# A list scheduler's margins, the place of the sine tables and a second engine for the first scalings, in a one-core attention, Fourier-mix and feed-forward kernel

## The chip, the cores and the metric

The kernel runs on one core of a Trainium2 chip. The metric is device time in microseconds (us) of one execution of the whole program. Three executions of the kernel before took 598.55, 597.87 and 601.43 us; the median is 598.55.

## The reference, cut to what matters

Eight batches, twelve heads, 448 tokens, head size 64 (model width 768), hidden width 3072, all float32. Attention uses normalised queries and keys and a temperature of 0.1. Its output goes through a two-dimensional Fourier transform of which the real part is added, a layer norm and a two-layer feed-forward part.

```python
q_n = q / (np.linalg.norm(q, axis=-1, keepdims=True) + 1e-06)
k_n = k / (np.linalg.norm(k, axis=-1, keepdims=True) + 1e-06)
attn = softmax(np.matmul(q_n, k_n.transpose(0, 1, 3, 2)) / tau)
x = (attn @ v).transpose(0, 2, 1, 3).reshape(8, 448, 768)
mixed = np.real(np.fft.fft(np.fft.fft(x, axis=1), axis=2))
u = x + mixed
un = (u - mean(u)) / np.sqrt(var(u) + 1e-06)
out = u + np.maximum(un @ w_ch1, 0.0) @ w_ch2
```

## The kernel before, in words

**Stages of a batch.** The program treats the batches one after another, with the attention of the next batch laid between the feed-forward matmuls of the present one. For a batch b:

- Loads. q and k come through the SP queue (line 646 for batches 0 and 1, line 772 into three staging buffers `STG` for the others), v through GpSimd's own queue (lines 829 to 832), and the weights w1 and w2 in 24 pieces through GpSimd's queue too (`W1b`, `W2b`, lines 578 and 579), at most three in flight: each waits for the third piece before it.
- Norms. ScalarE squares (`sq`, lines 653 and 781), VectorE sums per head (`ss`, 657 and 783), ScalarE takes the root as Ln and Exp (`ln`, `nrm`, 597 and 599), VectorE adds 1e-6 and takes the reciprocal (`eps`, `rcp`, 600 and 601). Then the scaling (`sc`): in batches 0 and 1 by VectorE (lines 679 and 683), from batch 2 on by GpSimd (line 790). In batches 0 and 1 TensorE transposes (`tk`, `tq`, `tt`, lines 707 to 732) and ScalarE or VectorE copies to `KT`, `QT`, `KTD` (`ek`, `eq`, `et`, lines 698 and 742); from batch 2 on DMA transposes do it on the SP queue (line 796), and `ktd` (a copy, line 1359 or 1360) and `qdup` (GpSimd, 821) follow them.
- Attention, in six pairs of heads. Scores by TensorE (`qk`, lines 869, 881, 882), exponentials by ScalarE (`ex`, 849; 24 instructions in batch 0), products with v (`pv`, 900 and 906), then on VectorE the reciprocal of the sums (`rd`, 924) and the product (`x`, 926).
- Fourier part. Sums and differences on VectorE (`fa`, `f`, `g`, lines 943 to 972), the transform over tokens on TensorE with a table `CSs` (and in batch 0 its negative `CSn`; `fs`, lines 988 and 993), copies (`te`, 1004 and 1005), the transform over the model width with a table `CSd` (`fd`, 1031), the additions (`u`, 1059) and the layer norm (`bs`, `ba`, `ln2`, `rs`, `un`, lines 1088 to 1097).
- Feed-forward. `h` (line 1163) and, after the relu copies (`relu`, 1179), the products with w2 (line 1194), the sums (1214 to 1226) and the stores.

**The tables.** `consts` makes the angles. Those for `CSs` are made first, on VectorE, and ScalarE turns them into sines at once (`sins`: 450 columns twice, lines 556 and 559), with the trigonometric function set loaded before anything else (line 349). The set with Ln and Exp is loaded right after the second square of batch 0 (`ldt0`, line 656). Two rows of `CSs` are halved by GpSimd (`half`, line 810) and `CSn` is made by VectorE (`sinn`, line 813). The angles of the larger table `CSd` are GpSimd's work (`tpd`, `tqd`, `trd`, `tad`, lines 504, 541, 546, 548) with a last step on VectorE (`tmd`, line 549). Its sines come after the last exponential of batch 0: the trigonometric set is loaded a second time, three sines follow (lines 556 to 559), and then the other set again (line 563).

**What sets the order.** Each engine runs its own instruction stream in order. The streams are written by a list scheduler in the program (`Plan.schedule`). Each step has a duration, a priority and its dependences; the scheduler takes the step that can start first by its own model of the engines and of the transfers (`FLOW`, `drain`), and by priority among equals. `SHIFT` adds hand-found numbers to the priorities of named steps. `rtime` gives the earliest start of a step: the end of each dependence, plus a fixed latency, plus the step's `margin`, which counts where TensorE takes the step or where the dependence is a transfer. `qk` has a margin of 0.3, `pv`, `fs` and `fd` of 0.2, the squares from batch 2 on of 1.0. `PIECE` and `PORT` model that a VectorE step of certain names waits for a piece of a GpSimd step that runs beside it. The model only sets the order; on the chip each step waits for the semaphores of its dependences.

**Fillers.** Where TensorE has a gap in the plan, `fill` puts in matmuls whose result is not used (line 1403), six at a time.

Of the kernel before, what the change touches and what calls it, by code (L numbers as in the profile page):

```python
# [13 lines left out]
DM = H * DH  # L14
# [23 lines left out]
    "ex3_0": {1: -3.7}, "tpd": {0: 1193.6}, "trd": {0: -57.8, 1: -108.8}, "tad": {0: -35.6, 1: -94.8}, "u1_0": {1: -264.8, 3: 72.4, 4: 79.2},  # L38
# [29 lines left out]
}  # L68

PIECE = {r"sc[KQ]\d_1": 0.95, r"scT\d_1": 0.42, r"sc\d_\d": 0.6, r"f[avm]\dp_\d": 0.54, r"t\d\d": 0.94}
PORT = r"eps\d|f[a01]\d_\d|g\d_\d|u\d+_\d|un\d_\d|s\d\d_\d|t\d\d|sc[KQT]\d_\d"

class Op:
# [1385 lines left out]
```

## Time and profile before

| | us |
|---|---|
| Median of three executions | 598.55 |
| The profiled execution, its own time | 598.88 |
| Its span, first to last instruction | 597.1 |
| TensorE busy, fillers included | 574.5 |
| Fillers (line 1403) before and after 53.15 us | 17.65 and 5.54 |
| First feed-forward matmul (line 1163) starts at | 53.15 |

The span lies 1.8 us below the profiled execution's own time. Times inside the profile are counted from the start of the span. In rows of the timeline the first number is the start, the second the duration, and a bracket at the end says how long the engine was idle before it and on whom it waited. PE is TensorE, PEld its weight load, DVE VectorE, ACT ScalarE, POOL GpSimd and SP the sync engine with its queue.

### The profile page before, as it was taken

The page shows a single profiled execution, that of the slowest core. Times are in us where ns is not written, and L with a number is a line of the kernel's source. Part 1 is how long each engine was busy: PE and PEld are TensorE (multiplying, and loading weights), DVE is VectorE, ACT ScalarE, POOL GpSimd, SP SyncE. Part 2 cuts the span into 40 slices and gives each one's busy share as a digit, 9 for nine tenths or more (in the row PEclk, how much of TensorE's full clock was granted, in tenths as well). Part 3 has the DMA queues.
Part 4 walks back from the last instruction along what each step waited for, and adds up shares of the span by engine and source line. Part 5 has one row for each costly group of instructions (what it writes and reads, how often), then busy time and mean ns, then how long its engine had stood idle before and what let it go on. Part 6 is the DMA issues. An engine that isn't in the chain of part 4 may idle for free.

```text
span 597.1 us, 15228 instructions
## 1 busy us (share of the span) xinstructions
PE 574.5 (96%) x6250; PEld 448.1 (75%) x6250; DVE 418.9 (70%) x976; ACT 354.8 (59%) x678; POOL 213.0 (36%) x324
## 2 busy tenths in 40 slices
PE   5889979999999999999999999999999999999997
PEld 4679867678678687678778688778668688778684
DVE  6968878898878776887788768865768556841222
ACT  7975878447867775468646676348745564124140
POOL 7843412732364264521460426341541210300302
PEclk9989999999999999999999999999999999999999
DMA  9999994964299349564592249373191210140001
GB/s 213 148 255 163 184 203 84 169 131 93 60 167 154 42 121 133 120 121 101 94 163 56 56 126 145 103 120 74 30 150 41 43 54 1 45 76 16 40 16 53
DMA packets 187638, 62.14 MB, mean 104 GB/s; under 512 B 166704, under 2 KB 185392, under 8 KB 187568
## 3 DMA queue, kind: packets, MB, share of 16 engines
q1 hardware_dynamic: 129648, 38.35, 34.1%
q0 software_dynamic: 57920, 22.81, 29.8%
q8 instruction: 49, 0.80, 0.6%
q14 instruction: 21, 0.17, 0.1%
HBM read 51.90 MB, written 11.01 MB: 105 GB/s over the span
## 4 chain that ended last, share of the span: by engine, by line
PE 84%; DMA 5%; DVE 3%; POOL 2%; ACT 2%; issue 1%; SPq 1%; ACTq 0%; POOLq 0%
PE PS L1163 34%; PE PS L1194 33%; PE PS L906 5%; PE PS L869 5%; PE PS L1031 2%; PE PS L993 2%; PE PS L900 2%; DMA VB<-in_v_dram 1%; DMA STG<-in_k_dram 1%; DMA QT<-QH 1%; SPq L772 1%; DMA W2b<-in_moe_w_ch_dram 1%; PE PS L881 1%; PE PS L1403 1%; DMA TX<-in_q_dram 1%
## 5 line engine op out<-in xcount | busy, mean ns | idle before, releaser
L1163 PE MATMUL PS<-UNT,W1b 128*128 128x256 bf16 (+1 forms) x2304 | 235.4, 259 | 2.6 <-ACT HQ L1179 1.2
L1163 PEld LDWEIGHTS PS<-UNT,W1b 128*128 128x128 bf16 x2304 | 198.3, 98 | 26.9 <-issue 3.7
L849 ACT ACTIVATE E<-PS 128x900 bf16<-128x900 f32 (+1 forms) x192 | 148.4, 829 | 36.3 <-PE PS L869 31.1
L1194 PE MATMUL PS<-W2b,HQ 128*128 128x384 bf16 x768 | 133.7, 326 | 0.0
L1179 ACT ACTIVATE HQ<-PS 128x512 bf16<-128x512 f32 x126 | 75.1, 597 | 84.8 <-PE PS L1163 84.1
L790 POOL TENSOR_TENSOR QH<-STG,SM 128x256 bf16<-128x256 f32 x126 | 79.0, 655 | 99.8 <-DVE SM L601 69.5
L1194 PEld LDWEIGHTS PS<-W2b,HQ 128*128 128x128 bf16 x768 | 73.4, 98 | 46.1 <-issue 1.9
L1219 POOL TENSOR_TENSOR OUTB<-OUTB,U 128x192 f32<-128x192 f32 x66 | 39.0, 611 | 147.6 <-ACT OUTB L1214 147.3
L1289 DVE TENSOR_TENSOR HQ<-HQ 128x512 bf16<-128x512 bf16 x141 | 61.3, 454 | 41.4 <-ACT HQ L1179 27.8
L1194 PE MATMUL PS<-TX,HQ 128*128 128x384 bf16 x396 | 70.6, 326 | 0.0
L1194 PEld LDWEIGHTS PS<-TX,HQ 128*128 128x128 bf16 x396 | 37.7, 98 | 24.4 <-issue 1.1
L783 DVE TENSOR_REDUCE SM<-QH 128x6 f32<-128x384 f32 x84 | 44.1, 538 | 12.5 <-ACT QH L781 12.4
L781 ACT ACTIVATE QH<-STG 128x384 f32<-128x384 f32 x84 | 42.7, 521 | 17.2 <-DMA STG<-in_k_dram 5.6
L906 PE MATMUL PS<-VB,E 128*128 128x65 bf16 x1152 | 51.9, 194 | 0.0
L906 PEld LDWEIGHTS PS<-VB,E 128*128 128x128 bf16 x1152 | 48.3, 98 | 1.3
L1248 POOL DMA_INDIRECT out_dram<-OUTB,IDX x20 | 21.0, 1052 | 67.8 <-DVE OUTB L1226 30.8
L869 PE MATMUL PS<-QT,KT 64*128 64x225 bf16 x576 | 39.5, 260 | 3.3 <-ACT E L849 3.2
L900 PE MATMUL PS<-VZ,E 128*128 128x130 bf16 x192 | 41.9, 221 | 0.3 <-ACT E L849 0.2
L1059 DVE TENSOR_TENSOR U<-ACG,X 128x384 bf16<-128x384 f32 (+3 forms) x70 | 38.6, 576 | 0.7
L1226 DVE TENSOR_TENSOR OUTB<-PS,OUTB 128x384 f32<-128x384 f32 x33 | 18.3, 556 | 28.3 <-PE PS L1194 27.0
L1179 DVE TENSOR_SCALAR HQ<-PS 128x512 bf16<-128x512 f32 x36 | 24.8, 688 | 17.3 <-PE PS L1163 16.9
L869 PEld LDWEIGHTS PS<-QT,KT 64*128 64x128 bf16 x576 | 22.8, 94 | 17.2 <-issue 6.5
(132 smaller groups left out, 648.1 us busy)
## 6 DMA issues: line engine op xcount, KB each, us to landing
STG<-in_q_dram SPq DMA_DIRECT2D x18, 384.0 KB, 3.8
STG<-in_k_dram SPq DMA_DIRECT2D x18, 384.0 KB, 4.3
VB<-in_v_dram POOLq DMA_DIRECT2D x24, 192.0 KB, 7.0
W1b<-in_moe_w_ch_dram POOLq DMA_DIRECT2D x12, 384.0 KB, 7.0
W2b<-in_moe_w_ch_dram POOLq DMA_DIRECT2D x12, 384.0 KB, 6.6
out_dram<-OUTB SPq DMA_DIRECT2D x7, 384.0 KB, 4.9
TX<-in_q_dram SPq DMA_DIRECT2D x2, 576.0 KB, 6.1
TX<-in_k_dram SPq DMA_DIRECT2D x2, 576.0 KB, 6.7
```

The source lines that it names most:

```text
L781: P.add("act", lambda a, sq=sq, src=buf[:, w * x:w * x + w]: a.activation(sq, src, ACTF.Square), t_act(w), pr, f"sq{i}_{b}", reads=bn, wri ...
L783: P.add("dve", lambda v, o=SS[:, i, H // ns * x:H // ns * (x + 1)], sq=sq: v.tensor_reduce(o, sq.rearrange("p (h d) -> p h d", d=DH), AX.X ...
L790: r = v.tensor_tensor(v3(qh)[:, h:h + 4], v3(buf)[:, h:h + 4], RN[:, i, h:h + 4].unsqueeze(2).to_broadcast((128, 4, DH)), AluOp.mult)
L849: return a.activation(o, self.PS[:, bk:bk + nc_, 0:SQ2], ACTF.Exp, scale=1.0 / self.tau)
L869: i = pe.matmul(self.PS[:, bk + h, c0:c0 + NK], self.KT[r, jj, kt * 128:(kt + 1) * 128], self.QT[r, jj, cols], start=True, stop=True)
L900: r = pe.matmul(o, st(6), self.VZ[:, j, :], start=not split, stop=(split and i == 0), skip_group_check=True)
L906: r = pe.matmul(o[:, 65 * h:65 * h + 65], st(2 * kt + h), self.VB[:, kt, 2 * j + h, :], start=(split and i == h == kt == 0), stop=((not sp ...
L1163: r = pe.matmul(self.PS[:, bk, x * n:(x + 1) * n], self.W1b[:, j, ft * 128:(ft + 1) * 128], self.UNT[:, j, cs], start=(j == 0), stop=(j == ...
L1179: return e.activation(o, i, ACTF.Relu) if e is self.nc.scalar else e.tensor_relu(o, i)
L1194: r = pe.matmul(self.PS[:, bk, 0:n], lhs(f), rhs(f), start=(start and f == 0), stop=(stop and f == NF // 2 - 1), skip_group_check=True)
L1219: r = g.tensor_tensor(self.OUTB[:, ob, xs], self.OUTB[:, ob, xs], self.U[:, ut, xs], AluOp.add)
L1289: P.add("dve", lambda v: v.tensor_tensor(cs(o), cs(a), cs(bq), op), 0.46, -0.5, f"{nm}{k}_{b}", reads=rd, writes=hr(o)(k))
```

## The change

Six things change.

1. **`LATE`.** A step can have a margin of another kind: behind a transfer the margin is now `late`, which for named steps is a number of the new table (`sq` of batch 2: 4.0, `sq` of batches 3 to 7: 2.0, `ktd` and `qdup`: 3.0, `qk` of batches 2 to 7: 1.5, `pv` of batches 2 to 7: 2.0, of batch 1: 1.0, `h` of batches 1 to 7: 0.3, `tmd`: 2.0) and for the others the old margin. Steps with a `late` of 1 or more have it behind GpSimd's steps too. The old margin of 1.0 of the squares is gone.
2. **Function sets and sine tables.** The program starts with the set that has Ln and Exp. All sines, those of `CSs` too, now come after all 24 exponentials of batch 0, behind one load of the trigonometric set; `half` and `sinn` follow them, and one load of the other set ends the group. The load `ldt0` after the second square is gone, and the squares of batch 0 no longer wait in the plan for the first sines. Loads of function sets: three in place of four.
3. **More engines for a step.** `half` may run on ScalarE or GpSimd, `sinn` on ScalarE, VectorE or GpSimd, `tmd` on ScalarE (as an absolute value) or VectorE. The first instances of the scalings (`sc` of batch 0) may run on GpSimd as well as on VectorE.
4. **Place in the program.** The angles of `CSd` are added before batch 0's attention, which changes their place among equal priorities; the old `SHIFT` entry of 1193.6 for `tpd` is gone.
5. **`PIECE`** names the scalings of batch 0 in place of those of batch 1.
6. **`SHIFT`** is replaced as a whole: every entry is new.

The amount of matmul work, the transfers and their sizes stay the same.

```diff
 SHIFT = {
-    "ix0": {0: 128.9}, "vz1": {1: 59.6}, "ld_q0_0": {0: -0.8}, "scT0_0": {0: 0.9}, "scK2_0": {0: -5.1}, "ek0_0": {0: 170.9}, "eq0_0": {0:
...
+    "iota": {0: -184.9}, "ix4": {0: 57.1}, "tad": {0: -260.6, 1: -488.3}, "tmd": {0: 18.4}, "half": {0: -0.8}, "ld_k0_0": {0: -42.8}, "ld_q0_0":
...
-PIECE = {r"sc[KQ]\d_1": 0.95, r"scT\d_1": 0.42, r"sc\d_\d": 0.6, r"f[avm]\dp_\d": 0.54, r"t\d\d": 0.94}
+LATE = {"tmd": 2.0, r"sq\d_2": 4.0, r"sq\d_\d": 2.0, r"ktd\d": 3.0, r"qdup\d": 3.0, r"qk\d._[2-7]": 1.5, r"pv\d\d_[2-7]": 2.0, r"pv\d\d_1": 1.0, r"h\d+_[1-7]": 0.3}
+PIECE = {r"sc[KQ]\d_0": 0.95, r"scT\d_0": 0.42, r"sc\d_\d": 0.6, r"f[avm]\dp_\d": 0.54, r"t\d\d": 0.94}
...
+        self.late = next((x for n, x in LATE.items() if re.fullmatch(n, name)), margin)
...
-                    t = max(t, d.end + (SEM_LAT if d.eng != "pe" else PE_LAT) + (op.margin if e == "pe" or d.dma is not None else 0.0))
+                    t = max(t, d.end + (SEM_LAT if d.eng != "pe" else PE_LAT) + (op.late if d.dma is not None or d.eng == "pool" and op.late >= 1 else op.margin if e == "pe" else 0.0))
...
-                    nc.scalar.preload_act_table_set("trig_and_small")
+                    nc.scalar.preload_act_table_set("natural_log_exp_and_others")
...
-                P.add("dve", lambda v, x=x, y=y: v.scalar_tensor_tensor(y, x, -1.0, x, AluOp.mult, AluOp.max), t_dve(NL), 30, "tmd",
+                P.add(("act", "dve"), lambda e, x=x, y=y: e.activation(y, x, ACTF.Abs) if e is self.nc.scalar else
+                      e.scalar_tensor_tensor(y, x, -1.0, x, AluOp.mult, AluOp.max), (t_act(NL), t_dve(NL)), 30, "tmd",
...
+        def tables():
+            self.trig = trig = P.add("act", lambda a: a.preload_act_table_set("trig_and_small"), 1.3, 10, "ldt0")
+            done = [table(ss, self.CSs, S, 2, 1, "s", 10, [trig], "CSs", 0)]
+            for p0, t in ((0, 0), (96, 1)):
+                row = self.CSs[p0:p0 + 1, t, 0, :]
+                P.add(("act", "pool"), lambda e, row=row: e.activation(row, row, ACTF.Copy, scale=0.5) if e is self.nc.scalar else
+                      e.tensor_scalar(row, row, 0.5, None, AluOp.mult), (0.35, 0.8), 10, "half", reads=["CSs"], writes=["CSs"])
+            P.add(("act", "dve", "pool"), lambda e: e.activation(self.CSn, self.CSs[:], ACTF.Copy, scale=-1.0) if e is self.nc.scalar else
+                  e.tensor_scalar(self.CSn, self.CSs[:], -1.0, None, AluOp.mult), (t_act(4 * NK), 0.5, 1.1), 10, "sinn", reads=["CSs"], writes=["CSn"])
+            done.append(table(sd, self.CSd, DM, 2, -1, "d", 10, [trig], "CSd", 0.8))
+            self.ldt = P.add("act", lambda a: a.preload_act_table_set("natural_log_exp_and_others"), 1.3, 10, "ldt", order=done)
...
-                if self.ldt is None:
-                    self.ldt = P.add("act", lambda a: a.preload_act_table_set("natural_log_exp_and_others"), 1.3, 9, "ldt0", order=[sqo])
...
-                    sc.append(P.add("dve", fn, t_dve(21 * n) if i < 2 else 0.3, pg[g] + 0.1 * j, f"sc{nm}{jj}_{b}", reads=names + [f"RN_{g}{i}"],
+                    sc.append(P.add("dve" if b else ("dve", "pool"), fn, ((t_dve(21 * n), 0.95) if i < 2 else (0.3, 0.42)) if b == 0 else t_dve(21 * n) if i < 2 else 0.3, pg[g] + 0.1 * j, f"sc{nm}{jj}_{b}", reads=names + [f"RN_{g}{i}"],
...
-                      t_act(w), pr, f"sq{i}_{b}", reads=bn, writes=sqn, margin=1.0)
+                      t_act(w), pr, f"sq{i}_{b}", reads=bn, writes=sqn)
...
+        self.args_d()
+        self.tables()
         self.attn(0)
-        self.args_d()
-        self.table_d([self.last_ex])
+        self.trig.order = tuple(self.exps)
```

More of the change, by code (lines that the diff above doesn't have):

```diff
@@ L79 @@
     __slots__ = ("engs", "eng", "fn", "durs", "prio", "deps", "raw", "start", "end",
-                 "idx", "acquire", "uses", "dma", "name", "seq", "margin", "serve", "order", "piece", "port", "flow")
+                 "idx", "acquire", "uses", "dma", "name", "seq", "margin", "serve", "order", "piece", "port", "flow", "late")
     def __init__(self, engs, fn, durs, prio, name, serve=0.0, margin=0.0):
@@ L561, in table @@
                          reads=[a + nm + x for a in ("tp", "tq") for x in ("01" if nm == "d" else [""])] + ["cst"], writes=[wr] + ["CSp"] * (nm == "d"), order=order)
-            if nm == "d":
-                P.add("act", lambda a: a.preload_act_table_set("natural_log_exp_and_others"), 1.3, pr, "ldt", order=[op])
-            return op
-        self.sin_s = table(ss, self.CSs, S, 2, 1, "s", -5, (), "CSs", 0)
-        self.table_d = lambda order: table(sd, self.CSd, DM, 2, -1, "d", 10, order, "CSd", 2.1)
+            return op
+        def tables():
[9 more added lines that the diff above has]
+            self.ldt = P.add("act", lambda a: a.preload_act_table_set("natural_log_exp_and_others"), 1.3, 10, "ldt", order=done)
+        self.tables = tables
     def weights(self, start):
@@ L597, in norms @@
         P.add("act", lambda a: a.activation(SS, SS, ACTF.Ln, bias=self.cst[:, 0:1]),
-              0.28, pr, f"ln{b}", reads=ssn + ["cst"], writes=ssn, order=[self.ldt])
+              0.28, pr, f"ln{b}", reads=ssn + ["cst"], writes=ssn, order=[self.ldt] if b else [])
         self.nrm = P.add("act", lambda a: a.activation(SS, SS, ACTF.Exp, scale=0.5), 0.17, pr, f"nrm{b}", reads=ssn, writes=ssn)
@@ L807, in attn @@
             self.norm(b)
-        if b == 0:
-            for p0, t in ((0, 0), (96, 1)):
-                P.add("pool", lambda g, p0=p0, t=t: g.tensor_scalar(
-                    self.CSs[p0:p0 + 1, t, 0, :], self.CSs[p0:p0 + 1, t, 0, :], 0.5, None, AluOp.mult),
-                    0.8, 30, "half", reads=["CSs"], writes=["CSs"])
-            P.add("dve", lambda v: v.tensor_scalar(self.CSn, self.CSs[:], -1.0, None, AluOp.mult), 0.34, 30, "sinn", reads=["CSs"], writes=["CSn"])
         if b > 1:
@@ L1371, in build @@
         self.stg_next = self.qh_next = self.ln_next = self.out_next = 0
[L1372 removed]
+        self.trs, self.loads, self.sqb, self.fd_ops, self.w, self.raw1, self.vl, self.pvs, self.exps = [], [], [], [], [], [], [], [], []
         self.first_st = self.main = self.last_qk = self.ldt = None
```

10 lines of the change are left out of this document (5 added, 5 removed), and 69 rows, old and new, of the table SHIFT.

## The prediction

> **What bounds the kernel now.** I read the page's head first, then the busy time by stretches, then the fillers' own row, and last the timeline round each place where TensorE stood still.
>
> ```profile
> span 597.1 us, 15228 instructions
> PE 574.5 (96%) x6250; PEld 448.1 (75%) x6250; DVE 418.9 (70%) x976; ACT 354.8 (59%) x678; POOL 213.0 (36%) x324
> ```
> ```profile
> 0.00:53.15 53.15, 41.42 (x597) 34.63 (x597) 40.34 (x95) 40.39 (x60) 32.54 (x59) 0.97 1.27 198
> 53.15:100.00 46.85, 42.65 (x600) 36.23 (x602) 38.47 (x85) 36.21 (x71) 16.38 (x23) 1.00 1.07 161
> 100.00:594.00 494.00, 490.47 (x5058) 377.25 (x5056) 340.05 (x797) 278.15 (x548) 164.07 (x242) 1.00 0.54 88
> ```
> ```profile
> 53.15:590.00 536.85, 5.54 (x84) 4.86 (x84) 1.00 0.59 95
> ```
>
> The second column of the stretches is their length, the third TensorE's busy time; the last fence is the same view for line 1403, the fillers, alone. From 53.15 us, the first feed-forward matmul, to 594 TensorE idles 46.85 - 42.65 = 4.20 and then 3.53 us, and 5.54 us of its work are fillers: 13.3 us of 541 can be won there, no more, since the change takes no matmul away. Before 53.15 us TensorE is not the bound; a chain of exponentials and VectorE steps is. So the change is worth what it takes from 53.15 us, plus its part of 13.3 us.
>
> Where the 13.3 us lie:
>
> ```profile
> 79.57 7.57 DMA STG<-in_k_dram
> ```
> ```profile
> 87.16 0.52 ACT L781 ACTIVATE QH<-STG 128x384 f32<-128x384 f32 x1 [3.93 <-DMA STG<-in_k_dram]
> 88.98 0.56 PE L869 MATMUL PS<-QT,KT 64*128 64x225 bf16 x8 [3.16 <-ACT E L849]
> ```
> ```profile
> 126.02 4.10 PE L1403 MATMUL PS<-W1b 128*128 128x128 bf16 x66
> ```
> ```profile
> 228.06 0.52 ACT L1359 ACTIVATE KTD<-QT 64x384 bf16<-64x384 bf16 x1 [2.13 <-DMA QT<-QH]
> ```
> ```profile
> 228.97 1.49 PE L1163 MATMUL PS<-UNT,W1b 128*128 128x256 bf16 x12 [0.70 <-DVE HQ L1179]
> 230.89 2.14 PE L1163 MATMUL PS<-UNT,W1b 128*128 128x256 bf16 x18 [0.43 <-ACT HQ L1179]
> ```
> ```profile
> 442.83 1.07 ACT L1359 ACTIVATE KTD<-QT 64x384 bf16<-64x384 bf16 x2 [7.97 <-DMA QT<-QH]
> ```
> ```profile
> 444.98 0.83 PE L1163 MATMUL PS<-UNT,W1b 128*128 128x256 bf16 x6 [0.76 <-ACT HQ L1179]
> ```
> ```profile
> 446.37 0.98 PE L993 MATMUL PS<-CS,ACG 128*65 128x225 bf16 x8 [0.56 <-DVE ACG L972]
> ```
>
> The reader is to see one pattern three times: a ScalarE step at the head of its in-order stream waits for a late transfer (3.93, 2.13, 7.97 us), what stands behind it (exponentials, relu copies) waits too, and TensorE runs dry for 3.16, 1.13 and 1.32 us: 5.6 us in all.
>
> **The change part by part.**
>
> *Margins (`LATE`).* They cost no instruction; they move the squares, `ktd`, first scores and products later in the streams. At 87.16 the square waited 3.93 us although the plan had a margin of 1.0 there; the new margin is 4.0 for just this batch, that is 3.0 more, so about 0.9 us of wait would be left, and TensorE's 3.16 exceeds what is left by far: I take the whole 3.16. Exponentials behind the square then start at once; next late is the square's own consumer, VectorE's sums and what follows them, for the scores of the batch after. For `ktd` the margin goes from 0 to 3.0 against waits of 2.13 and 7.97: I take the first, 1.13, whole, and of the second, 1.32, a quarter, 0.3, and give back 0.6 because a new order will have some new stall of the size of these. Sum 3.16 + 1.13 + 0.3 - 0.6 = 4.0 saved. Bounds: all 7.7 us of idle time after 53.15 saved, or 1 us lost, if the new order leaves the 3.16 and has a second stall like it in place of those of 1.13 and 1.32. The fillers of 4.10 us at 126 stand for a wait of batch 1's first feed-forward matmul on its layer norm; no margin touches that, I leave it in the sum at nothing and in the range at 4.1.
>
> *Start-up to the first exponential.*
>
> ```profile
> 8.71 1.28 ACT L656 ACT_TABLE_LOAD   x1
> 8.73 1.35 DVE L657 TENSOR_REDUCE SM<-E 128x18 f32<-128x1152 f32 x1 [0.41 <-ACT E L653]
> 10.43 0.29 ACT L597 ACTIVATE SM<-SM,MV 128x18 f32<-128x18 f32 x1
> 11.88 1.03 DVE L683 TENSOR_TENSOR QH<-TX,SM 128x384 bf16<-128x384 f32 x2
> 15.11 0.69 DVE L679 TENSOR_TENSOR TX<-TX,SM 128x128 bf16<-128x128 f32 x3
> 17.85 0.91 ACT L849 ACTIVATE E<-PS 128x900 bf16<-128x900 f32 x1
> ```
> ```profile
> L683 DVE TENSOR_TENSOR QH<-TX,SM x6: 546/553/558, 11.9 to 25.8; 128x384 bf16<-128x384 f32 x6
> ```
> ```profile
> L790 POOL TENSOR_TENSOR QH<-STG,SM x126: 602/612/1365, 94.0 to 449.1; 128x256 bf16<-128x256 f32 x126
> ```
> ```profile
> 18.22 3.79 POOL L504 TENSOR_SCALAR U<-OUTB,TX 128x192 f32<-128x192 f32 x4
> ```
>
> The removed load is 1.28 us of ScalarE, but not 1.28 us of the path: Ln at 10.43 needs VectorE's sum, which ends at 8.73 + 1.35 = 10.08. So Ln comes 0.3 us earlier, and the scalings with it. The two first sines (before the first square) fill a wait for k and q and give nothing. Then VectorE is full from 11.88 to 15.80 with six scalings of 0.553 us and three small ones. GpSimd can take some of the six: for 384 columns it needs 0.612 x 384/256 = 0.92 us each. Two taken off VectorE ahead of the first scores shorten its block by 2 x 0.55 = 1.1 us; as GpSimd's second ends later than VectorE's would have, I take 0.9. Sum 0.3 + 0.9 = 1.2 us saved. Bounds: 0.3 + 3 x 0.55 = 2.0 saved; 0.8 lost, if the two engines exclude each other for the whole instruction: a pair then takes 0.92 + 0.55 = 1.47 in place of 1.11, 0.36 more, for three pairs 1.1 lost, less the 0.3. I take the value near the good end, as the VectorE scalings, which go on to 25.8, vary only from 0.546 to 0.558 although GpSimd computed from 18.22 to 22.01. The Trainium skill, on its page SBUF — State Buffer, section "Who interferes with whom", speaks against this edit: a VectorE instruction with two inputs in SBUF and a GpSimd instruction that reads SBUF share a port pair, and the second to start blocks until the first has ended. No row here has two scalings side by side; by the rule the 0.9 becomes the loss of 1.1 and the sum below 2.0 us smaller. GpSimd's own queue gains 1.6 us ahead of the v loads, as `half` goes; v is not what the first products wait for, so this counts as nothing.
>
> *The exponentials of batch 0.*
>
> ```profile
> 31.49 0.56 DVE L549 SCALAR_TENSOR_TENSOR UNT<-U 128x385 f32<-128x385 f32 x1 [2.10 <-POOL U L548]
> 32.77 2.98 ACT L849 ACTIVATE E<-PS 128x450 bf16<-128x450 f32 x4 [2.19 <-PE PS L882]
> ```
>
> `tmd` held VectorE for 2.10 us waiting for GpSimd; behind it stood the `KTD` copy, on it TensorE's tail scores, and on them the next exponentials: ScalarE, which is the bound here, stood 2.19 us. With a margin of 2.0, with GpSimd's angles earlier in the program, and with ScalarE as a second choice, the step comes no longer ahead of its data; I take 2.1 us saved. Bounds: 0, if GpSimd's angles, now also behind scalings, are late again; 2.9, if the next idle stretches of ScalarE shrink as well. `tmd` on ScalarE, about 0.5 us twice, would lie behind the exponentials and ahead of the sines of `CSd`, which is not yet the end of the path (next part).
>
> *From the last exponential to the first feed-forward matmul.*
>
> ```profile
> 4.74 0.67 ACT L556 ACTIVATE CS<-UNT,MV 128x450 bf16<-128x450 f32 x1
> 5.31 0.56 ACT L559 ACTIVATE CS<-U 128x450 bf16<-128x450 f32 x1
> ```
> ```profile
> 40.21 1.28 ACT L556 ACT_TABLE_LOAD   x1
> 41.18 0.76 PE L988 MATMUL PS<-CS,F 128*128 128x225 bf16 x6
> 42.37 0.56 PE L988 MATMUL PS<-CS,F 128*128 128x225 bf16 x4
> 43.94 1.28 ACT L563 ACT_TABLE_LOAD   x1
> 44.26 0.98 PE L993 MATMUL PS<-CS,ACG 128*65 128x225 bf16 x8
> 46.63 0.85 PE L1031 MATMUL PS<-CS,E 128*128 128x193 bf16 x8 [0.39 <-ACT E L1004]
> ```
> ```profile
> L810 POOL TENSOR_SCALAR CS<-CS x2: 786/804/823, 7.1 to 9.4; 1x225 bf16<-1x225 bf16 x2
> ```
> ```profile
> 46.49 0.82 POOL L578 DMA_DIRECT2D W1b<-in_moe_w_ch_dram  x1 [3.34 <-DMA W1b<-in_moe_w_ch_dram]
> ```
> ```profile
> 50.42 0.29 ACT L1092 ACTIVATE MV<-MV 128x1 f32<-128x1 f32 x1 [3.85 <-DVE MV L1090]
> ```
>
> Now the table is ready long before; the first token transform (line 988) runs from 41.18 to 42.93 and the second (993) from 44.26 to 45.24. After the change `CSs` is there at 40.21 + 1.28 + 0.67 + 0.56 = 42.7, and with `half` at 0.8 us (one row on each engine) and `CSn` beside it at about 43.6. The second transform's data come at 44.26 as before; the first, 1.75 us, moves into 43.6 to 45.35, the second into 45.35 to 46.3, about 1.1 us later than 45.24. The sines of `CSd` take 43.94 - 41.49 = 2.45 now; they end at about 43.1 + 2.45 = 45.5, earlier than the transforms, and the copies after them need no function set. Of the 1.1 us I take 0.9 as lost, since the copy of the first result can now go ahead of the second's. The last load (1.28) falls into ScalarE's idle 3.85 us before 50.42: nothing; if that cover went, at most 1.28. Bounds: 0.4 lost, if `half` is all ScalarE's and the second transform goes first; 4.7 lost, if `half` lands on GpSimd behind a weight issue that waits, as at 46.49 for 3.34 us: ready at 47.3 + 2 x 0.8 = 48.9 in place of 43.6 is 5.3 later, less 0.6 that the start-up has already moved up. The weights themselves must not become late: their last piece is issued at 50.43 now, by GpSimd waiting for earlier pieces; the angles that held GpSimd go earlier, so I count nothing.
>
> *Sum.* 4.0 + 1.2 + 2.1 - 0.9 = 6.4 us saved of the profiled execution's 598.88: 592.5; that execution stands 0.3 above the median of 598.55, by which it is 592.2.
>
> **The rivals.**
>
> *The start is given back.* The scalings exclude each other (1.1 lost in place of 0.9 gained, by the port mechanism above) and the tables come late by 2 to 3 us: the first three edits outside the margins cancel, and only the 4.0 stays, less some new stall: 595.5. For it: GpSimd's wait of 3.34 us above. Against: the plan knows the waits for weights. The exclusion alone gives 592.2 + 2.0 = 594.2.
>
> *The new order also closes the 126 us gap.* The fillers' 4.1 us go besides: 592.2 - 4.1 = 588. For it: batch 1's whole attention moves up by 3.16 us when the stall at 88.98 goes, while the matmuls of batch 0 that lie beside it are fixed in number. Against: those matmuls move up as well.
>
> *The margins themselves cost.* Squares, `ktd`, scores and products of one batch lie in one chain, with 2.0 + 1.5 + 2.0 = 5.5 us of margins, so its layer norm ends up to 5.5 us later against TensorE's feed-forward work. What decides is the slack where a batch's first feed-forward matmul waits for its layer norm:
>
> ```profile
> 522.00 7.73 SPq L1118 DMA_TRANSPOSE UNT<-F  x4
> 534.45 0.82 PE L1163 MATMUL PS<-UNT,W1b 128*128 128x256 bf16 x6
> ```
>
> The transposes are issued by 529.73, and TensorE wants them at 534.45: 4.7 us, from which their landing still goes off. If all six later batches had so little, a delay of 5.5 would cost 1 to 3 us each, 12 in all: 592.2 + 12 = 604. It decides from 1.1 us lost per batch on (6.4/6). Against it: scores of one batch are spread over many microseconds of feed-forward work, and a margin moves only the first of them. *The change doesn't do what it says:* a square had a margin before and stood all the same; if transfers are later still than 4.0 us, the 4.0 goes and 596 stays.
>
> **How the numbers follow.** Within 1% means 592.6 to 604.5 here, about what a measurement tells from no change. My case (590 to 594, centre 592.2) has 0.44; the gap closed as well (586 to 590) 0.18; the start given back or the transfers later still (594 to 598.5) 0.25, of which 0.12 is the exclusion of the scalings, alone or with late tables; the margins cost 0.13, of which 0.09 above 604.5 or near it. About two thirds of my case lie below 592.6, so faster is 0.29 + 0.18 = 0.47, slower 0.09, same 0.44. The range 586.5 to 600.5 leaves out the last rival's larger part and the tips of the others.
>
> **What would show it.** First exponential at about 16.7 (now 17.85); no wait of VectorE on line 548; last exponential's end at 36.9 in place of 40.2; first matmul of line 1163 at about 50.7; no wait of TensorE over 1 us between 70 and 100, and none of ScalarE on `STG` loads over 1 us there. I am wrong if `half` stands behind weight issues on GpSimd, if GpSimd's scalings and VectorE's take turns, or if fillers of line 1403 grow after 53 us.

## The result and the profile after

Nine executions of the changed kernel gave a median of 595.36 us (594.32 to 603.46); nine of the kernel before beside them gave 599.12 (597.87 to 604.95). The ratio is 0.9923, with a 95% interval of 0.9894 to 0.9951: faster by about 0.8%, which is clear of the noise but less than 1%. The ratios here and below leave out executions that are more than 1.5% above the fastest of their kernel. The profiled execution took 595.36 us, its span is 593.6.

The page's head and TensorE's own line, after:

```profile
span 593.6 us, 15330 instructions
...
PE 577.2 (97%) x6304; PEld 450.6 (76%) x6304; DVE 424.8 (72%) x981; ACT 347.6 (59%) x667; POOL 218.9 (37%) x329
```

The busy time by stretches, cut at the first feed-forward matmul (now at 56.30 us, line 1170), and the same view for the fillers (now line 1411) alone:

```profile
0.00:56.30 56.30, 44.52 (x650) 37.12 (x651) 42.24 (x93) 38.47 (x57) 37.18 (x66) 0.97 1.22 195
56.30:100.00 43.70, 43.12 (x606) 36.50 (x607) 40.14 (x91) 37.29 (x71) 13.56 (x19) 1.00 1.09 157
100.00:590.50 490.50, 489.59 (x5053) 376.95 (x5050) 341.88 (x799) 271.86 (x539) 168.19 (x245) 1.00 0.54 89
```
```profile
56.30:593.60 537.30, 5.74 (x84) 4.83 (x84) 1.00 0.59 95
```

After the first feed-forward matmul TensorE now idles 0.58 + 0.91 = 1.49 us, where it idled 4.20 + 3.53 = 7.73. The fillers there stand as before (5.74 for 5.54). By stages, in us:

| | before | after | difference |
|---|---|---|---|
| first exponential starts | 17.85 | 17.82 | -0.03 |
| from there to the load of the function set behind the last exponential | 22.36 | 23.10 | +0.74 |
| from there to the first `fd` matmul | 6.42 | 8.04 | +1.62 |
| from there to the first feed-forward matmul | 6.52 | 7.34 | +0.82 |
| from there to the span's end | 543.95 | 537.30 | -6.65 |

So two results stand against each other: the start got 3.15 us longer, and the rest 6.65 us shorter.

The waits of TensorE over the whole span, longest sum first (line waiting, what it waited for, us in total, times, longest):

```profile
PE PS L1411 <- DVE TX L540: 4.4, 1, 4.4
PE PS L1411 <- DVE SM L669: 2.8, 1, 2.8
PE PS L719 <- POOL QH L695: 1.4, 1, 1.4
PE PS L876 <- ACT E L854: 0.6, 2, 0.4
PE PS L731 <- POOL TX L691: 0.6, 1, 0.6
```

The first two are fillers at the very start. The 3.16 us at 88.98 and the stalls at 229, 445 and 446 us have no successor above 0.6. The third and fifth rows are new: TensorE waits for scalings that are now made by GpSimd.

### The profile page after: what moved, and what is told of

It reads as the page before. It is cut to its first block, busy times and chain, and to the rows that moved or that the text cites. A ratio compares the mean times of both kernels' runs of the same rounds, so it can differ in the third digit from the quotient of the medians.

```text
span 593.6 us, 15330 instructions
## 1 busy us (share of the span) xinstructions
PE 577.2 (97%) x6304; PEld 450.6 (76%) x6304; DVE 424.8 (72%) x981; ACT 347.6 (59%) x667; POOL 218.9 (37%) x329
## 4 chain that ended last, share of the span: by engine, by line
PE 92%; ACT 3%; DVE 2%; POOL 2%; issue 1%; DMA 1%; POOLq 0%; ACTq 0%; DVEq 0%
PE PS L1170 37%; PE PS L1201 33%; PE PS L913 6%; PE PS L876 5%; PE PS L907 2%; PE PS L1000 2%; PE PS L1411 2%; PE PS L1038 2%; ACT E L854 1%; PE PS L888 1%; DMA TX<-in_q_dram 1%; PE PS L889 1%; POOL W1b L592 1%; POOL U L508 1%; DVE U L1066 1%
## 5 line engine op out<-in xcount | busy, mean ns | idle before, releaser
L1186 ACT ACTIVATE HQ<-PS 128x512 bf16<-128x512 f32 x116 | 69.4, 598 | 86.3 <-PE PS L1170 85.2
L802 POOL TENSOR_TENSOR QH<-STG,SM 128x256 bf16<-128x256 f32 x126 | 81.5, 674 | 97.1 <-DVE SM L615 79.6
L1296 DVE TENSOR_TENSOR HQ<-HQ 128x512 bf16<-128x512 bf16 x141 | 61.9, 461 | 42.9 <-ACT HQ L1186 26.9
L1186 DVE TENSOR_SCALAR HQ<-PS 128x512 bf16<-128x512 f32 x46 | 31.8, 691 | 23.8 <-PE PS L1170 23.2
L1066 DVE TENSOR_TENSOR U<-ACG,X 128x384 bf16<-128x384 f32 (+3 forms) x70 | 40.3, 597 | 0.8
L1221 ACT ACTIVATE OUTB<-PS 128x384 f32<-128x384 f32 x33 | 16.2, 492 | 41.9 <-PE PS L1201 38.4
```

The costliest lines, as they stand in the source:

```text
L802: r = v.tensor_tensor(v3(qh)[:, h:h + 4], v3(buf)[:, h:h + 4], RN[:, i, h:h + 4].unsqueeze(2).to_broadcast((128, 4, DH)), AluOp.mult)
L1066: return v.tensor_tensor(U[o0:o0 + n, ut, cs].rearrange("p (i e) -> p i e", e=2), src, X[i0:i0 + n, x, cs].rearrange("p (i e) -> p i e", e ...
L1186: return e.activation(o, i, ACTF.Relu) if e is self.nc.scalar else e.tensor_relu(o, i)
L1296: P.add("dve", lambda v: v.tensor_tensor(cs(o), cs(a), cs(bq), op), 0.46, -0.5, f"{nm}{k}_{b}", reads=rd, writes=hr(o)(k))
```

## The start, row by row

The way to the first exponential (fillers; Ln of batch 0; scalings on VectorE and GpSimd, line 695 for 384 columns, 691 for 128; transposes of k, copies to `KT`, transposes of q; the exponential):

```profile
7.94 5.55 PE L1411 MATMUL PS<-TX 128*128 128x128 bf16 x60 [2.76 <-DVE SM L669]
...
9.86 0.31 ACT L611 ACTIVATE SM<-SM,MV 128x18 f32<-128x18 f32 x1
...
11.09 1.03 DVE L695 TENSOR_TENSOR QH<-TX,SM 128x384 bf16<-128x384 f32 x2
...
12.64 0.84 POOL L695 TENSOR_TENSOR QH<-TX,SM 128x384 bf16<-128x384 f32 x1 [0.17 <-POOL IDX L530]
...
13.33 0.50 PE L719 MATMUL PS<-TX,QH 128*128 128x128 bf16 x6
...
13.70 1.02 DVE L710 CAST KT<-PS 128x384 bf16<-128x384 f32 x2 [1.43 <-PE PS L719]
...
15.07 0.72 POOL L691 TENSOR_TENSOR TX<-TX,SM 128x128 bf16<-128x128 f32 x1 [1.59 <-DVE SM L615]
...
15.93 0.49 PE L731 MATMUL PS<-TX 128*128 128x128 bf16 x3 [0.60 <-POOL TX L691]
...
17.82 0.92 ACT L854 ACTIVATE E<-PS 128x900 bf16<-128x900 f32 x1 [1.97 <-PE PS L876]
```

Ln is 0.57 us earlier than before, the first scaling 0.79. By the first exponential nothing is left of it, and the lead is gone before anything waits for GpSimd. The first transposes, whose data VectorE has ready at 11.09 + 1.03 = 12.12, stand behind 60 fillers that the plan put ahead of them, and start at 13.33; in the kernel before 48 fillers stood there, the data were ready at 12.91 and the transposes began at 12.94. VectorE then makes two of the `KT` copies, which ScalarE made before, so the reciprocal for the small scaling comes at 14.64 (13.37 before). GpSimd ends that scaling at 15.79, and the transposes of q wait for it.

Among the next exponentials TensorE waits for GpSimd again, and there one sees what two engines do to each other:

```profile
25.27 0.83 POOL L695 TENSOR_TENSOR QH<-TX,SM 128x384 bf16<-128x384 f32 x1
25.49 0.77 DVE L691 TENSOR_TENSOR TX<-TX,SM 128x128 bf16<-128x128 f32 x1
...
26.16 0.50 PE L719 MATMUL PS<-TX,QH 128*128 128x128 bf16 x3 [1.43 <-POOL QH L695]
...
27.19 2.55 ACT L854 ACTIVATE E<-PS 128x900 bf16<-128x900 f32 x3 [1.81 <-PE PS L876]
...
38.80 1.02 DVE L554 SCALAR_TENSOR_TENSOR UNT<-U 128x385 f32<-128x385 f32 x2
```

The first three small scalings took 0.69 / 3 = 0.23 us each before, on VectorE. Here one starts while GpSimd scales and ends at 26.26, just behind GpSimd's end at 26.10. TensorE waits 1.43 us for GpSimd and ScalarE 1.81 for TensorE. The last row is `tmd`: no wait any more.

Behind the last exponential (the load of the trigonometric set, `half` on ScalarE and on GpSimd, `sinn`, the first transform, the other load, the copy of the second transform):

```profile
40.92 1.28 ACT L570 ACT_TABLE_LOAD   x1
...
43.39 0.40 ACT L574 ACTIVATE CS<-CS 1x225 bf16<-1x225 bf16 x1
...
43.87 0.79 POOL L575 TENSOR_SCALAR CS<-CS 1x225 bf16<-1x225 bf16 x1 [4.26 <-ACT CS L574]
...
44.70 0.40 DVE L577 TENSOR_SCALAR HQ<-CS 128x900 bf16<-128x900 bf16 x1 [0.18 <-POOL CS L575]
...
45.15 0.77 PE L995 MATMUL PS<-CS,F 128*128 128x225 bf16 x6
...
47.47 1.35 ACT L1011 ACTIVATE E<-PS 128x900 bf16<-128x900 f32 x2
```

The two rows of `half` do not run side by side: GpSimd's waits for ScalarE's, and `sinn` for both, since the steps name one tile. The transform starts 45.15 - 40.92 = 4.23 us behind the load of the set.

Then the layer norm of batch 0 (VectorE's additions `u` and statistics):

```profile
49.84 1.95 DVE L1066 TENSOR_TENSOR U<-PS,X 128x384 bf16<-128x384 f32 x4 [1.48 <-PE PS L1038]
...
51.71 0.55 DVE L1095 BATCH_NORM_STATS2 ACG<-U 128x6 f32<-128x384 bf16 x1
...
54.22 0.46 DVE L1104 TENSOR_SCALAR F<-U,MV 128x768 bf16<-128x768 bf16 x1
```

Four additions go ahead of the first statistics, where before two did. The normalised rows start 54.22 - 48.96 = 5.26 us behind the first `fd` matmul; before it was 51.19 - 46.63 = 4.56.

## The experiments

To move single steps, the order of each engine's stream was written out in the kernel, and the scheduler takes only the head of each list; everything else is the program's own:

```diff
-                for op in ready[e]:
+                for op in line[e][at[e]:at[e] + 1]:
```

So the start of one kernel can be joined to the rest of the other, cut at the first feed-forward matmul. In the diffs below a line is one engine's stream. Each kernel has its own line numbers. "Rest" is the time from the first feed-forward matmul to the span's end.

**e1 and e2: start and rest exchanged.**

```diff
 e1: streams up to h0_0
-after's
+before's
 e2: streams from h0_0 on
-after's
+before's
```

> The engines' streams up to the first feed-forward matmul are those of the kernel before (its tables, its scalings, its order), everything after them stands in the order of the changed kernel. Theory A, start and rest are independent and the rest gains because no in-order stream stands behind a late transfer any more: first matmul of line 1163 at 53.2 us, from there 537.3 us as in the changed kernel, span 590.5, time about 592.2. Rival B, the rest gained because it starts 3.15 us later and its transfers have caught up by then: from the first matmul on 540 to 544 us, stalls behind transfers come back, time 595 to 599.

> The counterpart: the start of the changed kernel, the rest in the order of the kernel before. Theory A: first feed-forward matmul at 56.3 us, then 543.9 us with the stall of 3.2 us near 88 and the smaller ones near 230 and 444 again, time about 602. Rival B: the later start alone removes stalls, the rest takes 538 to 541 us, time 596 to 599.

e1: 594.54 us (593.7 to 603.61), ratio 0.9929 (0.9899 to 0.9959). e2: 603.3 (595.08 to 605.15), ratio 1.0031 (0.998 to 1.0083). In the profiles the rest of after takes 538.98 us behind the start of before, and the rest of before 546.74 behind the start of after. The gain belongs to the rest. But the two parts do not simply add: e1 begins the rest 3.08 us earlier than the changed kernel, and its span is only 1.4 us shorter (592.2). What is gained at the start is in part lost again behind it. And e2 shows a stall that is larger than any in the kernel before, ScalarE behind a staged load of batch 2:

```profile
93.57 0.52 ACT L918 ACTIVATE QH<-STG 128x384 f32<-128x384 f32 x1 [8.15 <-DMA STG<-in_k_dram]
```

**e3 and e4: single stalls taken out of the kernel before.**

```diff
 e3, ScalarE and VectorE
-sq0_2 sq0_2#1 ... ex3_1#2 ex3_1#3
+ex3_1#2 sq0_2 ex3_1#3 sq0_2#1        (and their sums ss0_2 behind relu18_0, x2_1)
 e4, besides
-ktd4 ktd7 where they were
+ktd4#1 behind relu20_2; ktd7 behind qe0_6; VectorE's ktd4 behind rcp4#3
```

> The kernel before with one local edit of its streams: the two squares of batch 2's tail, which waited 3.93 us for their load, stand behind four exponentials (about 4 us later) on ScalarE, and their sums (with the one that must follow them) likewise later on VectorE; nothing else moves. Theory A: TensorE's idle 3.16 us near 88 goes and stays gone, time 3.2 us below the kernel before, 595.7 against 598.9. Rival C, the order as a whole made the gain and a stall only moves on when one is taken out: TensorE idles as long elsewhere before 130 us or the fillers at 126 us must wait as well, gain under 1 us.

> As the run with the moved squares, and besides the KTD copies that waited for DMA transposes near 228 us (one on ScalarE, one on VectorE) and near 443 us (two on ScalarE) stand some 4 to 8 us later in their streams. Theory A: the three stalls of 3.16, 1.13 and 1.32 us are all gone, time 5.6 us below the kernel before, about 593.3; the rest, 5.6 of the 6.65 us that the changed kernel gained after its first feed-forward matmul, is then explained by late transfers alone. Rival C: not more than 1 us beyond the run with the squares alone.

e3: 598.43 (596.99 to 602.4), ratio 1.0003 (0.9972 to 1.0034). e4: 596.68 (594.67 to 601.97), ratio 0.9987 (0.9949 to 1.0026). Neither can be told from no change. TensorE's waits in e3:

```profile
PE PS L996 <- ACT E L976: 1.7, 1, 1.7
PE PS L1290 <- ACT HQ L1306: 1.5, 2, 1.1
```

The stall of 3.16 us between 80 and 100 became one of 1.70, and the later ones stayed. In e4 the one at 229 went, too, and the first one became 1.34; but near 440 ScalarE's wait of 7.97 us only moved from the `KTD` copies to the square that now stood ahead of them, where it is 8.68. TensorE still idled 3.85 us after the first feed-forward matmul (7.73 before, 1.49 after). The profiled execution of e4 is 3.2 us shorter than that of the kernel before, which its twelve executions together do not confirm. So taking out the stalls that the prediction names gives at most half of the idle time back; the rest of the gain is not in these places alone.

**e5: `tmd` behind its data, from e1.**

```diff
 VectorE
-tmd tmd#1 ... f10_0
+f10_0 tmd#1 tmd
```

> As the swap run (start of the kernel before, rest in the order of the changed kernel), with one edit: the two last steps of the large table's angles (tmd) stand behind the first sums of the Fourier part on VectorE, as the changed kernel has them, instead of ahead of the KTD copy. Theory: the 2.1 us that VectorE, TensorE and then ScalarE waited there are on the path; the last exponential ends near 38.1 in place of 40.2 and the first matmul of line 1163 starts near 51.1, time 592.5. Rival: the exponentials wait for something else as long; first matmul at 53 us, time 594.5.

The profiled execution took 591.94 us, with the first feed-forward matmul at 50.79 in place of 53.22: 2.43 us from this one wait. But the times fall into two groups, six from 591.14 to 595.18 and six from 599.4 to 601.74; the ratio is 0.9917 (0.9872 to 0.9961). With two groups neither a median nor a ratio says much, here and in e8; what parts them is looked for in e8 and tested by e9.

**e6, e7, e8: one part of the changed start each, put into e5.**

```diff
 e6, ScalarE, GpSimd, VectorE
-sins, half, sinn where before has them
+sins and half behind ex4_0#3; half#1 ahead of W1_10; sinn behind fa1_0#1
 e7, scalings of batch 0
-VectorE: scK1_0 scT0_0 scK5_0 scQ3_0 scQ5_0 scK4_0
+GpSimd: the same six
 e8, VectorE
-u0_0 u0_0#1 bs0_0 bs0_0#1 ...
+the order of u, bs, ba and un of the changed kernel
```

> As the run with the moved angles, with the sine tables made as in the changed kernel: the set with Ln and Exp first, no load behind the second square, all sines behind the last exponential, one row halved on ScalarE and one on GpSimd, the negative table on VectorE. Theory: nothing is won at the start (Ln waits for the sums in any case; first exponential 0 to 0.4 us earlier) and the token transform waits for its table, so the time from the last exponential to the first width transform grows from 6.4 to about 8 us; first matmul of line 1163 1.2 to 1.6 us later than in the run with the moved angles. Rival, as I predicted: 0.3 us won at the start and 0.9 lost here, 0.6 later.

> As the run with the moved angles, with the six scaling steps of batch 0 that the changed kernel gives to GpSimd (five large ones, one small) on GpSimd, in the places that it gives them in GpSimd's stream. Theory: they come late there, behind angles and weight issues, and TensorE's transposes of the second group wait for them; the first exponential is not earlier and the 24 exponentials stretch by 2 to 3 us or more; first matmul 2.5 us or more later than in the run with the moved angles. Rival 1, the shared port: scalings and VectorE steps take turns, VectorE's scalings last 0.9 us and more in place of 0.55. Rival 2, as I predicted: 0.9 us earlier.

> As the run with the moved angles, with VectorE's additions and statistics between the first width transform and the first layer norm in the order of the changed kernel (four additions ahead of the first statistics in place of two). Theory: the first layer norm comes 0.8 us later and the first matmul of line 1163 with it. Rival: this stretch is bound by TensorE's width transform, no change.

e6: 596.8 (593.79 to 598.62), ratio 0.9975 (0.9947 to 1.0004). The first exponential comes at 17.24 (e5: 18.31), and the load behind the last at 36.28 (37.28): about 1 us gained. The part behind it loses more: the first feed-forward matmul is at 55.89 (50.79), 5.1 us later. GpSimd's part of `half` stands behind a weight issue that waits, and `sinn` and the transform wait for it:

```profile
38.74 0.40 ACT L700 ACTIVATE CS<-CS 1x225 bf16<-1x225 bf16 x1
...
41.03 0.82 POOL L718 DMA_DIRECT2D W1b<-in_moe_w_ch_dram  x1 [5.78 <-DMA W1b<-in_moe_w_ch_dram]
41.92 0.79 POOL L701 TENSOR_SCALAR CS<-CS 1x225 bf16<-1x225 bf16 x1
42.75 0.40 DVE L703 TENSOR_SCALAR HQ<-CS 128x900 bf16<-128x900 bf16 x1 [2.94 <-POOL CS L701]
```

That is 41.92 - 39.14 = 2.8 us of queue which the changed kernel hasn't, and which comes from where I put the step; so e6 does not price the changed kernel's tables as they stand.

e7: 597.39 (596.9 to 604.22), ratio 0.9997 (0.9959 to 1.0034). First exponential at 19.63 (e5: 18.31), last one's end at 42.9 (37.27), first feed-forward matmul at 56.36: 5.6 us lost by six scalings on GpSimd. Most of that comes from their place in GpSimd's stream, as the expectation's own theory had it. A scaling that VectorE had done by 21.20 in e5 stands behind the angles and a weight issue here; the copy on VectorE and the exponentials on ScalarE wait for it, each through TensorE:

```profile
26.61 0.83 POOL L814 TENSOR_TENSOR QH<-TX,SM 128x384 bf16<-128x384 f32 x1 [0.17 <-POOL UNT L672]
...
27.87 0.56 DVE L829 CAST KT<-PS 128x384 bf16<-128x384 f32 x1 [4.41 <-PE PS L838]
...
29.14 1.36 ACT L980 ACTIVATE E<-PS 128x450 bf16<-128x450 f32 x2 [3.80 <-PE PS L1013]
```

A smaller part comes from steps of both engines at the same time. GpSimd's scaling of 384 columns and VectorE's small one beside it:

```profile
30.74 1.23 POOL L814 TENSOR_TENSOR QH<-TX,SM 128x384 bf16<-128x384 f32 x1
...
31.20 0.92 DVE L810 TENSOR_TENSOR TX<-TX,SM 128x128 bf16<-128x128 f32 x1
```

The small step takes 0.92 us in place of 0.23 and ends at 32.12, 0.15 us behind GpSimd's end at 31.97. Ahead of the first exponential a VectorE scaling of 384 columns takes 1.19 us in place of 0.55, beside GpSimd's that began at 13.65. What GpSimd takes off VectorE, VectorE there waits for.

e8: the normalised rows come 48.78 - 43.51 = 5.27 us behind the first `fd` matmul, like 5.26 in the changed kernel and unlike 4.56 in e5 (48.55 - 43.99); so that order is worth 0.7 us there. Little of it reaches the first feed-forward matmul, at 50.51: counted from the first `fd` matmul that is 7.00 us, and 6.80 in e5. The times: 600.84 (593.22 to 602.38), eight of ten above 600; ratio 1.0028 (0.9986 to 1.0069). Its profiled execution fell into the upper group and shows what sets it apart, in the chain of waits and the timeline:

```profile
78.03 15.54 DMA STG<-in_k_dram
```
```profile
93.59 0.52 ACT L911 ACTIVATE QH<-STG 128x384 f32<-128x384 f32 x1 [7.18 <-DMA STG<-in_k_dram]
...
95.79 0.94 PE L999 MATMUL PS<-QT,KT 64*128 64x225 bf16 x8 [6.75 <-ACT E L979]
```

A load of batch 2, issued at 78.03, lands at 93.57. In e5's profiled execution it was issued at 77.72 and its square had ended by 85.81, without a wait. ScalarE stands at that square for 7.18 us, the exponentials of batch 1 stand behind it, and TensorE loses 6.75. The stall costs more than its length: behind it the clock that TensorE was granted (the third number from the end) is 0.57 for 8 us, and 1.00 again afterwards.

```profile
94.00:102.00 8.00, 6.21 (x40) 4.28 (x42) 5.00 (x14) 5.61 (x12) 0.00 (x0) 0.57 0.00 0
102.00:597.60 495.60, 493.55 (x5106) 380.24 (x5102) 344.51 (x807) 274.67 (x544) 169.63 (x248) 1.00 0.51 89
```

After the first feed-forward matmul TensorE idles 8.5 us more than in e5, and its busy time is 2.3 us longer (536.13 for 533.82). Behind e2's stall of 7.38 us the clock was low, too (0.50 from 94 to 100 us); behind the 3.16 us in the kernel before it stayed at 1.00.

**e9 and e10: only the squares of that load moved later, in e5 and in the changed kernel.**

```diff
 ScalarE
-sq2_2 ex5_1 ex5_1#1 ln2 sq2_2#1 nrm2 ex4_1 ...
+ex5_1 ex5_1#1 ln2 nrm2 ex4_1 ... ex4_1#3 sq2_2 sq1_2#1 te0_1 sq2_2#1
 VectorE
-ss2_2 relu16_0#1 ... ss2_2#1 f00_1
+x4_1 ss2_2 ... g1_1#1 ss2_2#1 ktd2 ktd2#1 eps2#2 rcp2#2 fin00_0
```

> The order of e5 with one group moved: the squares of batch 2's third staged tile (128x384, the one whose load was landing at about 93 us in the execution of e8 and before 85 in that of e5) go on ScalarE from ahead of the exponentials of pairs 5 and 4 of batch 1 to behind the last of them, about 10 us later, and their sums and norms on VectorE go along, behind the feed-forward sums of batch 1. Nothing is computed differently. Theory A (the two groups of times of e5, 591 to 595 and 599 to 602, come from this one load, behind which ScalarE stood for 7 to 8 us): all executions come out in the lower group, median 591.5 to 592.5, none above 597, ratio to before 0.985 to 0.990; in the profile no ScalarE wait on a staged load over 1.5 us between 80 and 100 us. Theory B (the stall only moves on: another operation behind a late transfer, the first squares of the same batch or GpSimd's scalings, takes it over): still two groups, median 596 or above, with a ScalarE or GpSimd wait of 5 us or more named at another line. Theory C (the late load is only a sign of something slower as a whole, for instance of transfers that are all late): no two groups, but a median at 595 or above without any single wait over 3 us.

> The changed kernel with the same group moved in the same way. Theory A (with a start that ends at 56 us the late load is met in 1 of 9 executions only): the median stays at 594.8 to 595.6, and no execution is above 600; so this kernel is 3 us slower than e9, by the later start alone. Theory B: the moved squares cost something by themselves, median 596.5 or above, with TensorE idle time between 100 and 110 us that the changed kernel hasn't.

e9: 592.62 us, all six executions from 591.94 to 593.92, ratio 0.9891 (0.9841 to 0.9941). The upper group is gone, on another chip than e5's, where the kernel before scattered from 596.45 to 612.12. That the cause is met, and not merely absent, shows in its profile: the load is as late as in e8,

```profile
L902 SPq DMA_DIRECT2D STG<-in_k_dram x1: 4024/4024/4024, 77.9 to 77.9; - x1
...
DMA to landing us min/median/max: 15.5/15.5/15.5
```

and the moved squares start behind it, with no bracket, while the exponentials have gone ahead:

```profile
95.49 0.94 ACT L911 ACTIVATE QH<-STG 128x384 f32<-128x384 f32 x2
```

e10: 595.33 (594.69 to 596.57, twelve executions), ratio 0.9932 (0.9903 to 0.9961). The move costs nothing there, and no execution is above 597. Against e9, on the same chip, it is 2.7 us slower, although its first feed-forward matmul is at 56.72 in place of 50.30: of 6.42 us at the start less than half arrives at the end. Behind its earlier start e9 has 1.4 us more of idle time and 1.2 us more of fillers (6.93 for 5.70).

**e11 and e12: margins without the new shifts, and the new shifts without margins.**

```diff
 e11, in the kernel before
+LATE = {"tmd": 2.0, r"sq\d_2": 4.0, ...}     (with its rule in rtime)
 e12, in the changed kernel
-                    t = max(t, ... + (op.late if d.dma is not None or ... else op.margin if e == "pe" else 0.0))
+                    t = max(t, ... + (op.margin if e == "pe" or d.dma is not None else 0.0))
```

> The kernel before with the table of margins alone, planned anew: tables, scalings and the written shifts of issue times as before. Theory A (a margin is worth something only in an order that was searched with it; alone it puts the plan's work into an order that nobody tuned): slower than before, 603 or more, although the waits on late transfers are short (no ScalarE or VectorE wait on a staged load over 1.5 us); TensorE idle or filler time after the first feed-forward matmul over 20 us. Theory B (the margins by themselves bring the gain of the rest): 592 to 596, faster than before by about 4 us. Theory C (as in the prediction's rival that the margins themselves cost): 600 to 606, with idle time spread over the whole span.

> The changed kernel with the table of margins taken out and the single margin of 1.0 us of the squares put back, planned anew; its written shifts of issue times, late tables and shared scalings stay. It is the mirror of e11, where the margins alone gave 626.7 us. Theory A (margins and shifts are one thing: the shifts were found under the margins, and either without the other gives an order that nobody tuned): as far off as e11, 608 or more, with over 20 us of TensorE idle and filler time behind the first feed-forward matmul. Theory B (the shifts carry the gain and the margins are an ornament): 594 to 598, like the changed kernel. Theory C (the margins carry the gain, and the shifts only repair what the other edits moved): 598 to 604, with ScalarE waits on staged loads of several us as in the kernel before.

e11: 626.73 (625.05 to 627.51), ratio 1.0451 (1.0379 to 1.0523). e12: 619.78 (618.27 to 620.43), ratio 1.0312 (1.0209 to 1.0415). Their fillers after the first feed-forward matmul, e11 and then e12:

```profile
49.72:625.60 575.88, 28.37 (x450) 25.57 (x450) 0.99 0.55 90
```
```profile
57.46:617.40 559.94, 24.47 (x379) 21.73 (x378) 1.00 0.56 91
```

Fillers of 28 and 24 us in place of 5.7 mean gaps in the plan itself: the order that the scheduler finds is bad before any transfer is late. Margins alone don't even spare the late load; ScalarE waits 8.3 us for it in e11. So neither half of the change carries the gain alone. It is the order that the two give together. In particular "the margins brought 6.65 us" is not shown, and cannot be split further with these runs: whether shifts that are searched anew without the margins would do as well was not tried.

## Why the prediction was right in its time and wrong in its steps

The time (592.2 forecast, 595.36 measured) was inside the range and on the forecast side. It lies in the band of the rivals from 594 to 598.5, though, which had a chance of 0.25, and not in that of the case that was held likeliest. By the prediction's own bound of 1% it is no change (0.44) and not "faster" (0.47); the executions were steady enough to show the smaller gain. Of the profiled execution: 592.5 + 5.5 (start) - 2.65 (rest) = 595.4. Two errors of opposite sign lie in it, and that they nearly cancel is luck. Of the signs named in advance the waits came out as forecast (none on line 548's angles, none on staged loads or by TensorE over 1 us between 70 and 100), and the times did not: first exponential at 17.82 in place of 16.7, last one's end at 40.9 in place of 36.9, first feed-forward matmul at 56.30 in place of 50.7. GpSimd's scalings and VectorE's did take turns, a sign that was named for being wrong.

- *Margins: 4.0 saved; measured 6.65, between the value taken and the bound of 7.7.* The mechanism, streams in order behind late transfers, was right: idle time went from 7.73 to 1.49 (6.24 of the 6.65; the fillers took back 0.20, and the other matmuls were busy 0.6 less, which I did not trace). The step that failed is that I priced three stalls one by one in an otherwise unchanged order and gave 0.6 back for a new one. e3 and e4 show that stalls taken out singly in part move on, e11 and e12 that the order is not "the old one with steps shifted". I had costed the replaced `SHIFT` at nothing; without it the margins cost 4.5%.
- *Start to the first exponential: 1.2 saved; measured nothing (17.82 for 17.85).* Ln came 0.57 earlier, so the term for the function set was even too small; in e6, with the scalings left on VectorE, the first exponential comes 1.07 earlier. The failing step was the term of 0.9 for the scalings on GpSimd. In e7 they cost 1.32 us up to here, more than the bound of 1.1 - 0.3 = 0.8. In the changed kernel the fillers ahead of the transposes and the order on VectorE have a part in it, which was not separated. I took the value near the good end because VectorE's scalings of 384 columns had not varied beside GpSimd's angles. A small one had, in the kernel before:

```profile
23.98 1.25 POOL L541 TENSOR_SCALAR UNT<-U 128x385 f32<-128x385 f32 x2
24.78 0.58 DVE L679 TENSOR_TENSOR TX<-TX,SM 128x128 bf16<-128x128 f32 x1
```

It took 0.58 us where the one before it took 0.24, and ended at 25.36, 0.13 us behind GpSimd's step. The Trainium skill, page SBUF — State Buffer, section "Who interferes with whom", has the second of two such instructions wait until the first has ended; the traces agree to 0.1 to 0.2 us in the three pairs shown, and the prediction's own sentence on it was the better guide.
- *Exponentials: 2.1 saved; measured 0.74 lost.* `tmd`'s wait went as forecast, and e5 confirms its price (2.43 us, the forecast 2.1). But 1.43 and 1.81 us of waits for GpSimd's scalings took its place; I had costed them only up to the first exponential, and e7 shows that what they cost behind it is the larger part (4.3 of 5.6 us), for their place in GpSimd's stream.
- *Last exponential to the first `fd` matmul: 0.9 lost; measured 1.62.* Right mechanism. I had the two `half` rows on two engines at once, and `sinn` beside them; they run one behind the other, 0.40 + 0.79 + 0.40 us and the gaps. `half` did not stand behind a weight issue here, but e6 shows that it can, for 2.8 us.
- *First `fd` matmul to the first feed-forward matmul: not in the sum; 0.82 lost.* The normalised rows come 0.70 later, by VectorE's new order of additions and statistics. In e8 the same 0.7 cost only 0.2 at the first feed-forward matmul, so what makes up the 0.82 is not settled.
- *What the start gains counts in full:* assumed in the sum. Between e9 and e10 6.42 us at the start are 2.7 in the time.
- *The rival "the start is given back"* named 595.5, both of its mechanisms were met (the exclusion, late tables), and its time was right to 0.2. That is luck, too: it assumed 4.0 us for the margins less a new stall, and a start that comes out even, and it was met by a larger gain and a larger loss. *The 126 us gap* did not close (fillers 5.74 for 5.54). *The margins themselves cost:* not with the shifts that were found for them.

## What to carry to other kernels

A planned order is priced as a whole: a stall that is taken out alone can move on to the next wait, and a margin, or a set of hand-found shifts, was worth nothing here without the order found with it. When a start gets shorter, look at which transfers don't move up with it: here, with 2.4 us gained at the start, a late load cost about 9 us in half of the executions, until one group of steps was moved behind it. Behind a stall of 7 us TensorE's granted clock was lower, too. Before giving a second engine a share of a chain's work, look at every row in which both work at the same time, the short ones above all, and at where the steps would stand in the second engine's stream.

## What was not expected of the hardware

One load of 384 KB, issued at 77.0 to 78.0 us in e1, e5, e8 and e9, lands early or late by itself. In e1 this load and the one ahead of it, issued at 77.0 and 76.2, landed in 8.3 and 6.7 us:

```profile
DMA to landing us min/median/max: 6.7/7.5/8.3
```

In e8 and e9 it took 15.5. The issue on SP's queue itself took 2.2 to 2.8 us in e1 and e5 and 4.0 to 4.1 in e8 and e9; but in e6 it took 4.1 as well, at 78.6, and the square of that load began by 90.1 without a wait, so a long issue does not by itself go with a load of 15.5. Weight pieces of the same size are under way beside it on GpSimd's queue and land in 7 us either way. The Trainium skill, page DMA: Bandwidth & Descriptors, section "Queues, rings and completion order", has each DMA engine take turns between the queues that it has work for; that alone would make the load about as slow as the pieces beside it, as in e1, and not 15.5. What decides between the two was not found. It fits that the times of the kernel before scatter, too (from 594.7 to 612 over all its executions), but that was not traced.
